# Whole V and U products for the first batch, and a new order of words for the first two batches

## The chip, the core and the metric

The kernel runs on one core of one Trainium2 chip. Its time is the device time of one execution in microseconds (us); less is better. The core's engines work side by side, each through its own list of instructions in order: TensorE (matmuls; PE in the profile), VectorE (DVE), ScalarE (ACT), GpSimd (POOL), and SyncE (SP), which here only issues transfers. An engine waits when an operand or a buffer is not ready, and everything behind the waiting instruction in its list waits too.

## The reference

Attention with grouped heads feeds a gated feed-forward block, for 8 batches of 384 tokens. There are 16 query heads and 4 key/value heads of 64 elements; the 1024 outputs of the heads of a token form its row of x.

```python
scores = scale * np.matmul(q, k.transpose(0, 1, 3, 2))
attn = np.exp(scores) / sum(...)            # softmax over keys
x = np.matmul(attn, v)  -> (batch, 384, 1024)
h = np.maximum(x @ w_in, 0.0)               # 1024 columns
u, v = h[..., :512], h[..., 512:]
v_n = (v - mean(v)) / sqrt(var(v) + 1e-6)
v_s = einsum('ts,bsd->btd', w_spatial, v_n) + b_spatial
out = (u * v_s) @ w_out
```

Inputs and outputs are 32-bit floats in device memory; the kernel multiplies in 16-bit floats and accumulates in 32 bits.

## The kernel before, in words

The work of a batch is cut into small steps, and the order in which they are issued is written out by hand as strings of words; `play` (line 641) reads a string and calls the step of each word from the table STEPS (line 592). The first list, RAMP, loads the first inputs. START (line 652) plays all of batch 0, nearly all of batch 1 and most of batch 2. STEADY (line 665) is played for each batch from 3 on, interleaving a batch with the end of the two before it. LAST finishes. The order of words fixes the order of instructions on every engine: there is no reordering behind it. A word belongs to batch 0 in START, to batch 1 with one `+`, to batch 2 with `++`, to batch 3 with `+++`.

The words, with b the batch, gp (0 or 1) the half of the heads, and t, tq, st one of three tiles of 128 tokens:

- `lq`, `lk`, `lv`: SyncE loads q of a half (line 223), k (line 178), v (line 191). `wv`, `wu`, `wo`: GpSimd issues loads, with conversion to 16 bits, of the v half of w_in's columns, its u half (line 137), and w_out (line 144); digit 0 is the first 512 rows of w_in, 1 the others. `ws` loads w_spatial and the bias, `cws` converts them on GpSimd (lines 157, 160), `tws` turns them with a transfer (line 166).
- `cq`, `ck`, `cv`: GpSimd converts q, k, v to 16 bits (lines 247, 184, 197). For batch 0 some pieces are converted on VectorE: `cqv<gp><qd><half>` (pair qd of four query heads, one half) and `ckv1` (k of the second half of the heads). The 32-bit load buffers exist once each (pool `ld`), so `lk+` can be issued only when batch 0's k has been converted, `ckv1` included.
- `K`, `Q`, `Qj`, `Qh`: TensorE turns k or some columns of q, and VectorE copies the result to SBUF (lines 278 to 297). From batch 2 on this is done by transfers: `tk` (line 263), `tq` (line 269). For batch 1, `Q10+` turns the first third of q of the second half of the heads and reads what both casts of `cq1+` wrote.
- `s<n>` (18 per batch, 9 per half of the heads): two score matmuls into two PSUM banks (line 315). `e<n>`: ScalarE's exponential of them (line 329).
- `X<gp><tq>`: 24 matmuls of attention weights and v (line 342). `N<gp><tq>`: VectorE divides by the sums and writes x (lines 356, 357).
- `T<tq>`: SyncE turns one tile of x by a transfer (line 368); `Tp<gp><tq>` does half a tile of it on TensorE, with a copy on VectorE (lines 378, 379). Batch 0 uses `Tp`, the others `T`.
- `V<st>`: x times the v half of w_in, for one tile of tokens, 8 matmuls over the 1024 rows (line 113), and then relu (line 434). `S<st>`: mean and variance (lines 447, 448). `rs`: reciprocal deviation on ScalarE (452, 453). `vn`: the three normalised tiles (line 461). `p<m>`: times w_spatial, three matmuls, and the bias added (line 492). `U<m>`: x times a quarter of the u half, 8 matmuls, and gating (line 505). `O<i>`: 4 matmuls with w_out, a copy (line 525), and for every second one a store (line 533).
- `A<st>` and `H<m>`, for batch 0 alone: the first half of V and U. Four of the eight matmuls, those over the first 512 rows, are done early; VectorE copies the half product to SBUF (lines 414, 423). The later `V` or `U` of that tile then does the other four, and VectorE adds the kept half (lines 436, 503) before relu (line 437) or gating.
- `w<n>`: n idle matmuls on a constant tile (line 303).

PSUM has 8 banks. `take1` and `take2` give a word the bank, or pair of banks, that was released longest ago; a word therefore also waits for the reader of the bank's former content.

TensorE at `V0+` waits for `T0+`. SyncE issues transfers in the order of the words: before the change `tk++ tq0++ tq1++ T0+ lk+++ lq0+++ T1+`.

Of the kernel before, what the change touches and what calls it, by code (L numbers as in the profile page):

```python
# [17 lines left out]
def kernel(  # L18
# [622 lines left out]
    def play(b, text):  # L641
# [8 lines left out]
    RAMP = """  # L650
        lqj00 lkga0 lqj01 lqd01 lt lkg1 lqd10 lv lqd11"""
    START = """
        w28 cqjv00 cka0 Qj00 w4 Ka0 w5 cqjv01 Qj01 w7 cqp011 wv0 cqv010 s0 s2 cv wv1 lk+ lq0+ Qh01 cqv100 ckv1
        cqv111 s1 e0 lq1+ ws s3 lv+ w9 s5 e2 ck+ e1 cqv101 s4 e5 e4 w6 cq0+ cqv110 s7 wu0 Q10 K1 cq1+ cws Q11
        s8 e7 e3 wu1 tws s10 lk++ s6 s9 e6 e8 lq0++ e10 X00 X01 e9 lq1++ lv++ N00 s11 N01 e11 s13 X02 e13 N02
        s12 cv+ Tp00 X10 wo e12 N10 Tp01 K0+ A0 Tp10 Q12 s14 e14 A1 V0 X11 Tp02 s15 N11 s16 K1+ A2 s17 e16
        Tp11 Q00+ S0 e15 e17 V1 X12 N12 s1+ Q10+ Q01+ Tp12 e1+ s0+ s9+ e0+ S1 e9+ s10+ ck++ H0 Q11+ Q02+ V2
        s2+ e10+ S2 e2+ s11+ rs s3+ e3+ H2 s4+ vn e11+ cq0++ H1 e4+ X00+ cq1++ tk++ N00+ p1 X10+ s5+ tq0++
        tq1++ N10+ T0+ p0 H3 e5+ U0 s12+ e12+ s7+ Q12+ U1 p2 s13+ s14+ e7+ p3 e13+ cv++ X01+ N01+ e14+ U3 s6+
        lk+++ U2 s17+ X11+ e17+ e6+ N11+ lq0+++ T1+ s8+ V0+ O4 e8+ X02+ N02+ s2++ S0+ e2++ lq1+++ s15+ O5 s0++  # L660
        e0++ s1++ O0 e15+ s16+ e16+ O2 lv+++ e1++ O1 V1+ O3 s11++ X12+ e11++ s9++ ck+++ e9++ N12+ T2+ S1+
        s10++ X00++ N00++ e10++ s14++ cq0+++ X10++ s3++ s5++ N10++ e5++ s4++ e4++ V2+ e3++ cq1+++ s13++ e14++
        tk+++ s12++ tq0+++ s8++ tq1+++ e13++ X01++ S2+ rs+ e12++ T0++ e8++ vn+ N01++ s7++ X11++ N11++ e7++ p1+
        p2+ p0+ V0++ cv+++ s15++ s17++ s6++ e6++ U0+ e15++ X02++ s16++ N02++ S0++ e17++ e16++ T1++ U1+"""
    STEADY = """
        s2 s1 e2 s0 e0 U2'' X12' p3'' N12' lq0+ cq0+ e1 lk+ s11 lq1+ e11 U3'' s9 tq0+ s10 s4 e9 e10 O0'' X00
        N00 ck+ V1' X10 S1' e4 s5 s3 T2' e5 lv+ e3 N10 O1'' V2' S2' s14 s13 s12 e13 T0 e12 O2'' O3'' X01 e14
# [45 lines left out]
```

## Time and profile before

| | |
|---|---|
| runs (median of 4; lowest to highest) | 257.55 us (256.96 to 258.83) |
| profiled execution: its time, its span | 258.83 us, 257.1 us |
| TensorE busy | 237.8 us (93%) |
| VectorE busy | 173.4 us (67%) |
| ScalarE busy | 143.7 us (56%) |
| GpSimd busy | 46.9 us (18%) |
| mean granted TensorE clock | 0.986 |

The span runs from the first to the last instruction; the profiled execution's own time has 1.7 us around it. Busy time is summed per engine. In the page's rows of slices each digit is the busy share of one fortieth of the span in tenths. A line of the timeline gives start, length, engine, line of the kernel, operation, the tiles written and read, the number of instructions, and in brackets how long the engine had been idle and what ended that. The lengths of matmuls overlap, so the time that one takes in a row is read from start to start.

### The profile page before, as it was taken

Reading aid. Unit: us, or ns where it says so; the run is one execution under the profiler, and the core shown is the slowest. Engines: PE = TensorE matmul, PEld = TensorE weight load, DVE = VectorE, ACT = ScalarE, POOL = GpSimd, SP = SyncE. Lnnn points to the kernel's source line nnn. Section 1 sums busy time; section 2 is a strip of 40 time slices with the busy share of each in tenths; the row PEclk is TensorE's granted clock in tenths of the full one; section 3 lists DMA queues with packets and bytes.
Section 4 is the critical chain, followed back from the end, with each engine's and each line's share of the span. In section 5 each row is a group of like instructions: output and inputs, shape, how many; then the busy total and the mean of one; then the engine's idle time right before and its main releaser. Section 6 shows DMA issues by size and latency. Waiting matters only on the chain.

```text
span 257.1 us, 5788 instructions
## 1 busy us (share of the span) xinstructions
PE 237.8 (93%) x2395; PEld 129.6 (50%) x2395; DVE 173.4 (67%) x350; ACT 143.7 (56%) x164; POOL 46.9 (18%) x72
## 2 busy tenths in 40 slices
PE   7779888919988999999999999999999999999993
PEld 6346435504354555455544654465446554565671
DVE  2538999913665656776677667875696667776963
ACT  3993576721669476584577474748476666800000
POOL 1615911423300061000610043003310000000000
PEclk9999999986999999999999999999999999999999
DMA  6999899989668694597977797789886325320254
GB/s 209 238 264 315 129 171 252 244 182 282 220 189 164 158 254 102 171 212 212 231 195 209 176 271 200 179 167 294 182 215 163 30 45 165 123 41 0 113 214 167
DMA packets 78042, 47.20 MB, mean 184 GB/s; under 512 B 47168, under 2 KB 74176, under 8 KB 78016
## 3 DMA queue, kind: packets, MB, share of 16 engines
q1 hardware_dynamic: 74880, 43.36, 65.5%
q0 software_dynamic: 2720, 3.15, 8.1%
q8 instruction: 18, 0.29, 0.5%
q10 hardware_dynamic: 416, 0.33, 0.4%
q14 instruction: 8, 0.07, 0.1%
HBM read 25.95 MB, written 12.58 MB: 150 GB/s over the span
## 4 chain that ended last, share of the span: by engine, by line
PE 72%; DMA 18%; POOL 4%; ACT 2%; SPq 1%; DVE 1%; issue 1%; POOLq 0%; DVEq 0%; ACTq 0%
PE banks L113 52%; DMA q<-in_q_dram 12%; PE banks L315 10%; PE banks L342 10%; DMA xT<-x 3%; POOL q L247 2%; DMA v<-in_v_dram 2%; ACT aT L329 2%; DMA k<-in_k_dram 1%; POOL setup L157 1%; POOL w_in L137 1%; POOL v L197 0%; SPq L269 0%; DVE bn L447 0%; POOL bias_tp L160 0%
## 5 line engine op out<-in xcount | busy, mean ns | idle before, releaser
L329 ACT ACTIVATE aT<-banks 128x1024 f16<-128x1024 f32 x144 | 137.8, 1025 | 77.0 <-PE banks L315 69.2
L113 PE MATMUL banks<-w_in,xT 128*128 128x512 f16 x192 | 47.4, 390 | 7.3 <-DMA xT<-x 5.7
L113 PE MATMUL banks<-w_out,gT 128*128 128x512 f16 (+1 forms) x196 | 48.0, 381 | 0.0
L342 PEld LDWEIGHTS <-aT 128*128 128x128 f16 x1152 | 40.9, 98 | 13.3 <-ACT aT L329 5.9
L113 PE MATMUL banks<-xT,w_in 128*128 128x384 f16 (+1 forms) x320 | 47.3, 294 | 0.0
L315 PE MATMUL banks<-qT,kT 64*128 64x512 f16 x288 | 44.5, 381 | 2.2 <-ACT aT L329 0.7
L342 PE MATMUL banks<-v,aT 128*128 128x65 f16 x1152 | 43.2, 193 | 3.0 <-ACT aT L329 3.0
L247 POOL CAST q<-q 128x768 f16<-128x768 f32 (+1 forms) x29 | 23.5, 837 | 103.6 <-DMA q<-in_q_dram 66.1
L525 DVE COPY osb<-banks 128x512 f32<-128x512 f32 x47 | 32.0, 687 | 10.4 <-PE banks L113 9.9
L113 PEld LDWEIGHTS <-w_in 128*128 128x128 f16 x320 | 25.6, 98 | 17.5 <-issue 5.7
L357 DVE TENSOR_TENSOR x<-banks,rec 128x512 f16<-128x512 f32 x48 | 33.2, 691 | 1.7
L434 DVE TENSOR_SCALAR v_r<-banks 128x512 f32<-128x512 f32 x21 | 14.5, 692 | 27.5 <-PE banks L113 27.5
L113 PEld LDWEIGHTS <-xT 128*128 128x128 f16 x192 | 18.3, 99 | 29.0 <-DMA xT<-x 6.9
L113 PEld LDWEIGHTS <-gT 128*128 128x128 f16 x196 | 17.1, 99 | 24.9 <-issue 10.0
L315 PEld LDWEIGHTS <-kT 64*128 64x128 f16 x288 | 12.1, 94 | 24.8 <-issue 19.0
L505 DVE SCALAR_TENSOR_TENSOR gT<-banks,vs 128x384 f16<-128x384 f32 x24 | 13.4, 558 | 11.7 <-PE banks L113 11.7
L492 DVE TENSOR_TENSOR vs<-banks,bias_tp 128x384 f32<-128x384 f32 x28 | 14.9, 553 | 6.6 <-PE banks L113 6.6
L113 PE MATMUL banks<-wsT,v_n 128*128 128x384 f16 x96 | 19.3, 326 | 0.0
L447 DVE BATCH_NORM_STATS2 bn<-v_r 128x6 f32<-128x512 f32 x24 | 16.5, 689 | 0.4
L356 DVE RECIPROCAL rec<-banks 128x8 f32<-128x8 f32 x48 | 9.7, 202 | 9.2 <-PE banks L342 8.0
L461 DVE TENSOR_SCALAR v_n<-v_r,mv,rstd 128x512 f16<-128x512 f32 x24 | 11.6, 541 | 0.8 <-ACT rstd L453 0.6
L113 PEld LDWEIGHTS <-v_n 128*128 128x128 f16 x96 | 8.0, 98 | 6.2 <-issue 2.3
(49 smaller groups left out, 91.7 us busy)
## 6 DMA issues: line engine op xcount, KB each, us to landing
out_dram<-osb SPq DMA_DIRECT2D x22, 512.0 KB, 2.9
q<-in_q_dram SPq DMA_DIRECT2D x14, 768.0 KB, 7.9
v<-in_v_dram SPq DMA_DIRECT2D x8, 384.0 KB, 4.4
k<-in_k_dram SPq DMA_DIRECT2D x7, 384.0 KB, 6.2
w_in<-in_moe_w_in_dram POOLq DMA_DIRECT2D x8, 256.0 KB, 6.7
q<-in_q_dram SPq DMA_DIRECT2D x8, 192.0 KB, 4.3
w_out<-in_moe_w_out_dram POOLq DMA_DIRECT2D x2, 512.0 KB, 12.4
out_dram<-osb SPq DMA_DIRECT2D x3, 256.0 KB, 2.1
```

The lines of the kernel that those rows point to most:

```text
L113: nc.tensor.matmul(dst[c : c + cols], w[:, c : c + cols], m, start=(i == 0), stop=(i == n - 1))
L247: engine(columns(b, gp, T["q16", b, gp])[:, js, :, half, :], T["q32", b, gp][:, half, js, :].rearrange("p j (t d) -> p j t d", t=NST),)
L315: nc.tensor.matmul(banks[:, xs[half], :], T["kT", b][lo:hi, t, gp, :], rhs[lo:hi, c * 512 : (c + 1) * 512], start=True, stop=True,)
L329: nc.scalar.activation(T["aT", b, gp, c][:, t, :, :], banks[:, x : y + 1 : y - x, :], AF.Exp, scale=scale)
L342: nc.tensor.matmul(banks[:, xs[half], j * (D + 1) : (j + 1) * (D + 1)], aT[:, t, half, o : o + P], T["v16", b][:, 2 * gp + half, t, 0 : D ...
L357: nc.vector.tensor_tensor(T["x16", b, tq][:, gp], ps[:, :, :, 0:D], rec.to_broadcast([P, 2, G, D]), ALU.mult)
L434: nc.vector.tensor_scalar(v_r, banks[:, x, :], 0.0, None, op0=ALU.max)
L447: nc.vector.bn_stats(bn, T["v_r", b, st])
L461: engine.tensor_scalar(v_n, T["v_r", b, st], T["mv", b][:, st, 0:1], T["rstd", b][:, st : st + 1], op0=ALU.subtract, op1=ALU.mult,)
L492: nc.vector.tensor_tensor(vs, f32(x, S), bias_tp, ALU.add)
L505: nc.vector.scalar_tensor_tensor(T["gT", b][:, mu, :], src, 0.0, T["vs", b, mu], op0=ALU.max, op1=ALU.mult)
L525: copy(osb[:, half * 512 : (half + 1) * 512], banks[:, x, :])
```

## The change

Only the string START is changed; RAMP, STEADY and LAST and all functions stay.

- The words A0, A1, A2, H0, H1, H2, H3 are gone. V0 to V2 and U0 to U3 of batch 0 find no kept half and do all eight matmuls in one accumulation, with relu or gating straight from PSUM, as for all other batches.
- All other words are the same ones in another order, but for the idle matmuls: w9 and w6 are gone, w3 and w22 are new.
- On SyncE the order becomes `tk++ T0+ tq0++ tq1++ lk+++ lq0+++ T1+`; for batch 2, `tk+++ T0++ tq0+++ tq1+++`; the three stores of batch 0 come in another order and lv+++ before them. GpSimd's list is the same as before. On both, the v half of w_in is loaded ahead of the u half.
- On VectorE ckv1 comes after cqv110 and cqv101 instead of after cqv100.
- On TensorE Q10+ comes ahead of V0, K0+ ahead of Tp00, O4 ahead of V0+, X10+ ahead of the first p.

```diff
     START = """
-        w28 cqjv00 cka0 Qj00 w4 Ka0 w5 cqjv01 Qj01 w7 cqp011 wv0 cqv010 s0 s2 cv wv1 lk+ lq0+ Qh01 cqv100 ckv1
-        cqv111 s1 e0 lq1+ ws s3 lv+ w9 s5 e2 ck+ e1 cqv101 s4 e5 e4 w6 cq0+ cqv110 s7 wu0 Q10 K1 cq1+ cws Q11
-        s8 e7 e3 wu1 tws s10 lk++ s6 s9 e6 e8 lq0++ e10 X00 X01 e9 lq1++ lv++ N00 s11 N01 e11 s13 X02 e13 N02
-        s12 cv+ Tp00 X10 wo e12 N10 Tp01 K0+ A0 Tp10 Q12 s14 e14 A1 V0 X11 Tp02 s15 N11 s16 K1+ A2 s17 e16
-        Tp11 Q00+ S0 e15 e17 V1 X12 N12 s1+ Q10+ Q01+ Tp12 e1+ s0+ s9+ e0+ S1 e9+ s10+ ck++ H0 Q11+ Q02+ V2
-        s2+ e10+ S2 e2+ s11+ rs s3+ e3+ H2 s4+ vn e11+ cq0++ H1 e4+ X00+ cq1++ tk++ N00+ p1 X10+ s5+ tq0++
-        tq1++ N10+ T0+ p0 H3 e5+ U0 s12+ e12+ s7+ Q12+ U1 p2 s13+ s14+ e7+ p3 e13+ cv++ X01+ N01+ e14+ U3 s6+
-        lk+++ U2 s17+ X11+ e17+ e6+ N11+ lq0+++ T1+ s8+ V0+ O4 e8+ X02+ N02+ s2++ S0+ e2++ lq1+++ s15+ O5 s0++
+        w28 cqjv00 cka0 Qj00 w4 Ka0 w5 cqjv01 Qj01 w7 cqp011 wv0 cqv010 cv wv1 lk+ s0 s2 lq0+ lq1+ w3 e0 s1 e1
+        Qh01 s4 ws cqv110 cqv101 s5 ckv1 cqv100 e2 cqv111 lv+ ck+ cq0+ e4 wu0 cq1+ w22 s8 s7 e5 e7 s6 Q11 s3
+        K1 Q10 cws s9 e6 wu1 e3 e8 tws lk++ e9 s10 lq0++ X00 X01 s11 N00 lq1++ s13 lv++ e10 N01 e11 cv+ X02
+        N02 X10 wo s12 s14 e13 N10 K0+ Tp00 Q12 e14 Tp01 e12 s15 s16 Tp10 e15 X11 Q10+ N11 V0 Tp11 K1+ s17
+        Q00+ e17 e16 Tp02 S0 V1 X12 s9+ S1 s1+ s0+ N12 e9+ s10+ e1+ Tp12 Q01+ ck++ e10+ V2 s11+ S2 s2+ e0+ s3+
+        e2+ Q11+ Q02+ s4+ rs X00+ cq0++ e11+ vn cq1++ e4+ X10+ e3+ tk++ N00+ p2 N10+ T0+ p0 s5+ s13+ s7+ e5+
+        s12+ p1 tq0++ e12+ tq1++ e7+ e13+ U0 U1 X01+ N01+ cv++ Q12+ p3 U3 s14+ s17+ U2 s6+ lk+++ e14+ lq0+++
+        e17+ X11+ s8+ e6+ N11+ T1+ e8+ O4 V0+ X02+ N02+ O2 s2++ e2++ lq1+++ O0 s1++ e1++ s16+ lv+++ O3 O1 S0+
...
```

The rest of START, to the end of batch 2's share, is reordered in the same way; the words in it are the same.

## The prediction

> **What bounds the kernel now.** I read the page's engine table and its slices first, then TensorE's waits, then the timeline of TensorE around the longest wait, then SyncE's and GpSimd's timelines to see what that wait hung on, last the busy time by stretches.
>
> ```profile
> PE 237.8 (93%) x2395; PEld 129.6 (50%) x2395; DVE 173.4 (67%) x350; ACT 143.7 (56%) x164; POOL 46.9 (18%) x72
> ...
> PE   7779888919988999999999999999999999999993
> ...
> PEclk9999999986999999999999999999999999999999
> ```
>
> TensorE is busy for 93% of the span. Its idle 19.3 us lie in the first third and in the tail: the stretches give it full business from 86 to 180 us and from 200 to 240. So the body is TensorE's own work, and the change, which alters no word after START, can win or lose only in when TensorE leaves START. That is at 90.97 us (three scores in a row, the first of STEADY). The 166.1 us behind it I take as fixed.
>
> ```profile
> PE banks L113 <- DMA xT<-x: 5.7, 1, 5.7
> PE banks L342 <- ACT aT L329: 3.0, 5, 0.9
> PE banks L113 <- DVE xT L379: 1.1, 1, 1.1
> ```
>
> One wait of 5.7 us stands out. TensorE's timeline shows it, and what it costs afterwards:
>
> ```profile
> 50.93 0.39 PE L315 MATMUL banks<-qT,kT 64*128 64x512 f16 x2
> 57.06 3.59 PE L113 MATMUL banks<-w_in,xT 128*128 128x512 f16 x8 [5.74 <-DMA xT<-x]
> 60.45 1.91 PE L113 MATMUL banks<-w_out,gT 128*128 128x512 f16 x4
> 62.15 0.95 PE L342 MATMUL banks<-v,aT 128*128 128x65 f16 x24
> ```
>
> V0+ waits until 57.06. Its 8 matmuls then take 3.39 us up to O4's start (1.73 later in the trace), and O4's 4 take 1.70 (0.97 later). The granted clock (the column after POOL's, stretches of half a microsecond) says why:
>
> ```profile
> 54.50:55.00 0.50, 0.00 (x0) 0.00 (x0) 0.00 (x0) 0.00 (x0) 0.00 (x0) 1.00 1.12 204
> 55.00:55.50 0.50, 0.00 (x0) 0.00 (x0) 0.00 (x0) 0.00 (x0) 0.00 (x0) 0.94 1.04 209
> 55.50:56.00 0.50, 0.00 (x0) 0.00 (x0) 0.00 (x0) 0.00 (x0) 0.00 (x0) 0.50 1.10 208
> ...
> 62.00:62.50 0.50, 0.50 (x11) 0.34 (x10) 0.10 (x1) 0.00 (x0) 0.34 (x1) 0.73 1.24 326
> ```
>
> It falls to half at 55.4 and is back at 62.3. This costs 1.66 + 0.73 = 2.4 us. The wait is for T0+, the transfer that turns x of batch 1's first tile. SyncE shows why it is late:
>
> ```profile
> 28.74 1.33 SPq L166 DMA_TRANSPOSE wsT<-setup  x1
> ...
> 44.02 3.92 SPq L263 DMA_TRANSPOSE kT<-k  x1
> 49.17 4.36 SPq L269 DMA_TRANSPOSE qT<-q  x2
> 53.62 1.57 SPq L368 DMA_TRANSPOSE xT<-x  x1
> ```
>
> x was complete at 43.16 (VectorE's second product for that tile). T0+ stood in SyncE's queue behind tq0++ and tq1++, and tq1++ waited for GpSimd's cast cq1++, which waited for the last q load of batch 2.
>
> **The change, part by part.**
>
> *T0+ moves ahead of tq0++ and tq1++.* Only tk++ is still before it, whose issue ends at 47.94. T0+ then lands between 47.94 + 3.4 = 51.3 (its own latency before) and 54.1, where tq0++ landed from about that place (49.17 + 4.9), because kT's transfer ahead of it landed only at 52.9 (44.02 + 8.9). I take 54.0. tq0++ and tq1++ come 1.6 us later for it. Their readers, the scores of batch 2, stand behind V0+ and five output words, so that is hidden; so is T1+, still behind tq1++ and two loads: 54.8 + 6.6 (its latency before) = 61.4, against V1+ at some 65.
>
> *A0 to A2 and H0 to H3 go.* VectorE loses lines 414, 436, 423 and 503 (2.1 + 2.1 + 2.2 + 2.2 us), and line 437's 2.7 becomes three of line 434 at 0.692: 9.2 us in all. VectorE was 92% busy from 20 to 50 us, but TensorE waited for it only 1.8 us there (1.1 for xT, 0.7 for x). The matmuls stay 8 a tile, so TensorE is given nothing back but some 0.1 us per split; what counts is that they run later. Between X10 and Q12 and up to Tp02 A0, A1 and V0 filled 0.87 + 1.74 us.
>
> *Q10+ moves ahead of V0, and nothing covers it.* X11 ended at 24.97; without these 2.6 us TensorE is at Q10+ at about 22.4. Q10+ needs cq1+:
>
> ```profile
> 21.97 1.60 POOL L247 CAST q<-q 128x768 f16<-128x768 f32 x2 [4.72 <-DMA q<-in_q_dram]
> 23.51 1.43 POOL L137 DMA_DIRECT2D w_in<-in_moe_w_in_dram  x2
> 24.94 1.61 POOL L247 CAST q<-q 128x768 f16<-128x768 f32 x2
> 26.47 2.24 POOL L157 CAST setup<-ws 128x384 f16<-128x384 f32 x3
> ```
>
> That ends at 26.55 at the earliest: a new wait of 4.1 us where there was work. Behind it in TensorE's queue stand V0, Tp11, V1, and in VectorE's the copy of Q10+, with N11 after it.
>
> *ckv1 moves behind cqv110 and cqv101.* lk+ reuses the k buffer that ckv1 reads; it was issued at 9.18, just after ckv1. cqv110 needs the second q pair, issued at 4.86 with 5.1 to landing: 9.96. Two casts and ckv1 (3 x 0.44) later it is 11.3, so lk+, lq0+, lq1+ start 2.1 us late. Ends: at 0 the engines were full anyway, at 2.1 all passes on to cq1+. The row is the stretch table: DMA share 1.06 to 1.17 in every 2 us from 8 to 22. The Trainium skill, "DMA: Bandwidth & Descriptors", Queues, rings and completion order, says that each DMA engine takes turns between the queues that have work; then GpSimd's w_in loads use what SyncE leaves, the same bytes are through by 22, and the slip would be near 0. By the issue times alone it is 2.1. SyncE's own queue was moving the q pair until 10.5, so it is empty only 10.5 to 11.3; I take 0.7. GpSimd's chain cq0+, wu0, cq1+, cws, and SyncE's tws and all behind it, slip with it. So cq1+ ends at 27.25 and the wait is 4.8 us.
>
> *From there.* Q10+ 0.3, V0 1.75: 29.3. Then VectorE sets the pace up to V2: v_r 0.69, four copies 1.6, statistics 0.87, v_r 0.69, statistics 0.87, N12 0.86 = 5.6, to 34.9; s10+, Tp12 and Q01+ 0.8; the copy of Tp12 0.4; V2 1.75: 37.8. v_r and statistics 1.56, two copies 0.8, v_n 1.46 (ScalarE's rstd lies beside the copies): 41.6. The first p starts at 41.7; before it was at 40.65. From it to the end of s8+ were 10.6 us of TensorE without a gap. Now come three H's worth more (3 x 0.70), O4 (0.97), less X10+ (0.75, now earlier) and 0.4 for the splits, plus some 0.6 for banks that wait for N10+ and vs: V0+ and O4 are through at 41.7 + 10.6 + 2.1 + 0.97 - 0.75 - 0.4 + 0.6 + 1.75 = 56.6. V0+ is reached at 54.8, and T0+ lands at 54.0 + 0.7 = 54.7: the wait is gone, the clock stays up. X02+ starts at 56.6 instead of 62.15: 5.5 us won.
>
> *The rest of START* has the same words for 28.8 us, with 2.4 us of waits (0.39, 0.49, 0.30, 0.53, 0.66), most on exponentials and banks. A changed order can make that 0.5 to 4.5; I leave it. w22, w3 instead of w9, w6: 10 more idle matmuls at 0.068 (line 303's nine took 0.61). They lie in 8.9 to 10.4, where ScalarE's exponentials, 0.93 apart from 6.83, are the pace up to X00: hidden. Without that cover they are 0.7 us.
>
> *The clock in the new wait.* Row: TensorE stopped at 51.3, and the clock fell 4.1 us later; by that a wait of 4.8 us loses it, and 2.4 us with it. The Trainium skill, "TensorE: Matmul & The Clock Gate", Part 1, says that the clock is judged over free-running windows of 3.4 us; a wait of 4.8 us holds a whole one in (4.8 - 3.4)/3.4 = 4 of 10 cases (an estimate from that page). The trace's 55.4 and 62.3 are 6.9 apart, two such windows, so I follow the rule: likeliest no loss, 2.4 us kept for the range.
>
> **Sum.** 258.83 (the profiled execution; span 257.1) - 5.5 = 253.3. That execution was the slowest of four, 1.28 above the median. If its excess was the half clock alone, 253.3 stands; if it is spread, 252.0. I take 253.0, which is 4.6 under the median 257.55 (1.8%).
>
> **The rivals.**
> - *The clock falls in the wait for cq1+*: 253.0 + 2.4 = 255.4. For it speaks the 4.8 us, against it the windows.
> - *T0+ lands late all the same*, as T1+ did with 6.6 us to landing: 48.6 + 1.6 + 6.6 = 56.8 instead of 54.8: about 255, still without the half clock.
> - *Slower: the load behind cq1+.* Place: Q10+, with the whole of batch 0's V behind it. Each microsecond by which lq0+ and lq1+ land later is one on TensorE and on every transfer behind tws. It decides from 0.7 + 4.6 = 5.3 us of slip, or 2.9 with the clock lost too. If the w_in loads, 2.1 us ahead, hold the engines until they are done (they landed at 19.5 and 20.9), two q loads of 768 KB at some 300 GB/s, 2.6 us each, come after: slip 4 to 5, with the clock lost about 259.5. Against it speaks the turn-taking.
> - *More than forecast*: no slip, fewer bank waits in the rest of START: 250.8.
> - *The change does nothing*: if the three other executions had no wait at T0+, there would be little to win: 257. They lie 0.4 to 0.7% below the profiled one; without the wait and the half clock they would lie 8.1 us, 3%, below it.
>
> **How the numbers follow.** Likeliest 0.46 (251.5 to 254.5); clock lost 0.17; T0+ late 0.11; more 0.08; slower 0.12; nothing 0.06. The range 250.3 to 257.0 leaves out the slower case, the half of nothing, and some of the low end. What a measurement can tell from no change is about 0.5%, 1.3 us. Faster: 0.46 + 0.15 + 0.09 + 0.08 = 0.78; same: 0.02 + 0.02 + 0.06 = 0.10; slower 0.12.
>
> **What would show it.** Right: no wait for xT over 1 us at V0+, the clock full at 52 to 62, xT's transfer directly behind kT's on SyncE; a wait of 4 to 6 us of line 292 for GpSimd's q cast near 22 us; lk+ issued near 11.3; VectorE busy some 164 us; STEADY from about 85.5. Wrong: TensorE at V0+ later than 57, STEADY from 90 or later, or new waits of several microseconds between 57 and 85.

## The result, and the profile after

The changed kernel takes 255.89 us (median of 43 executions, 252.36 to 258.44); the kernel before, in 64 executions beside it, takes 256.31 us (253.07 to 258.87). The ratio is 0.9992, 95% interval 0.9967 to 1.0017: no difference that can be measured, where 253.0 us and a gain of 1.8% were forecast. (Ratios in this document are of the executions within 1.5% of each kernel's fastest; medians are of all executions; where the two differ, both are given.)

The profiled execution of the changed kernel took 253.93 us, its span 252.2 us. Read against the prediction it looks like a success, and that is the puzzle of this case. The engine table and the slices of the page after:

```profile
PE 236.3 (94%) x2405; PEld 130.6 (52%) x2405; DVE 165.1 (65%) x336; ACT 143.9 (57%) x164; POOL 45.8 (18%) x72
...
PEclk9999799999999999999999999999999999999998
```

VectorE lost 8.3 us, and the row of the clock has no dip any more at 51 to 64 us, but a new one in its fifth slice. TensorE's waits up to 90 us:

```profile
PE banks L292 <- POOL q L247: 2.9, 1, 2.9
PE banks L315 <- DVE x L357: 2.2, 3, 1.1
```

The 5.7 us for xT are gone, and the wait for GpSimd's cast of q that the prediction put there is the longest now. SyncE's own queue (start, length, line, operation):

```profile
41.74 4.03 SPq L263 DMA_TRANSPOSE kT<-k  x1
45.86 2.08 SPq L368 DMA_TRANSPOSE xT<-x  x1
47.99 4.87 SPq L269 DMA_TRANSPOSE qT<-q  x2
```

T0+ is issued at 45.86, directly behind the transfer of k, and lands 5.7 us later, at 51.6. TensorE's timeline at Q10+ and V0, at V0+, and at the end of START (the last line is the first three scores of STEADY):

```profile
25.73 0.61 PE L292 MATMUL banks<-ident,q 128*128 128x128 f16 x4 [2.85 <-POOL q L247]
26.13 3.29 PE L113 MATMUL banks<-w_in,xT 128*128 128x512 f16 x8
...
55.10 1.89 PE L113 MATMUL banks<-w_in,xT 128*128 128x512 f16 x8
56.83 0.89 PE L342 MATMUL banks<-v,aT 128*128 128x65 f16 x24
...
85.23 1.09 PE L315 MATMUL banks<-qT,kT 64*128 64x512 f16 x6
```

V0+ no longer waits, X02+ follows at 56.83, and START is left at 85.23, where 85.5 was forecast. So in this one execution START ends 5.7 us earlier than in the profiled execution of before, and the two executions are 4.9 us apart (253.93 and 258.83). The medians differ by 0.4 us. The profiled execution of before stands 2.5 us above its kernel's median, that of the changed kernel 2.0 us below its own: most of the 4.9 us lies in which executions were profiled. The experiments ask what each part of the change does to the time.

### The profile page after: what moved, and what is told of

Same layout as the page of the kernel before. It is cut to its first block, busy times and chain, and to the rows that moved or that the text cites. A ratio compares the mean times of both kernels' runs of the same rounds, so it can differ in the third digit from the quotient of the medians.

```text
span 252.2 us, 5789 instructions
## 1 busy us (share of the span) xinstructions
PE 236.3 (94%) x2405; PEld 130.6 (52%) x2405; DVE 165.1 (65%) x336; ACT 143.9 (57%) x164; POOL 45.8 (18%) x72
## 4 chain that ended last, share of the span: by engine, by line
PE 81%; DMA 6%; DVE 5%; ACT 3%; POOL 2%; issue 1%; SPq 0%; DVEq 0%; ACTq 0%
PE banks L113 56%; PE banks L315 12%; PE banks L342 12%; DMA q<-in_q_dram 5%; ACT aT L329 2%; DMA xT<-x 1%; DVE bn L447 1%; POOL q L247 1%; DVE x L357 1%; PE banks L292 1%; DVE v_r L434 1%; POOL w_in L137 1%; DVE osb L525 1%; DVE rec L356 0%; PE banks L378 0%
## 5 line engine op out<-in xcount | busy, mean ns | idle before, releaser
L113 PE MATMUL banks<-w_in,xT 128*128 128x512 f16 x192 | 46.8, 388 | 1.0 <-ACT aT L329 1.0
L113 PE MATMUL banks<-w_out,gT 128*128 128x512 f16 (+1 forms) x196 | 47.1, 376 | 0.0
L113 PE MATMUL banks<-xT,w_in 128*128 128x384 f16 (+1 forms) x320 | 46.6, 294 | 0.0
L247 POOL CAST q<-q 128x768 f16<-128x768 f32 (+1 forms) x29 | 22.9, 817 | 100.3 <-DMA q<-in_q_dram 82.7
L434 DVE TENSOR_SCALAR v_r<-banks 128x512 f32<-128x512 f32 x24 | 16.6, 692 | 20.0 <-PE banks L113 20.0
L505 DVE SCALAR_TENSOR_TENSOR gT<-banks,vs 128x384 f16<-128x384 f32 x28 | 15.6, 558 | 14.3 <-PE banks L113 14.3
```

Source lines behind the costliest of these rows:

```text
L113: nc.tensor.matmul(dst[c : c + cols], w[:, c : c + cols], m, start=(i == 0), stop=(i == n - 1))
L247: engine(columns(b, gp, T["q16", b, gp])[:, js, :, half, :], T["q32", b, gp][:, half, js, :].rearrange("p j (t d) -> p j t d", t=NST),)
L434: nc.vector.tensor_scalar(v_r, banks[:, x, :], 0.0, None, op0=ALU.max)
L505: nc.vector.scalar_tensor_tensor(T["gT", b][:, mu, :], src, 0.0, T["vs", b, mu], op0=ALU.max, op1=ALU.mult)
```

## Experiments

Each was timed beside the kernel before on the same chip; rows with different times in the column "before beside it" are of different chips and times. "START left" is the start of the first scores of STEADY in the profiled execution, "rest" is its span minus that. The number of idle matmuls (the words w) is listed because it turned out to matter.

| kernel | idle | median us (n) | before beside it | of medians | ratio, 95% | START left | rest |
|---|---|---|---|---|---|---|---|
| before (the profile shown ahead) | 59 | | | | | 90.97 | 166.1 |
| before_again | 59 | 254.89 (1) | 256.57 | | | 87.29 | 165.8 |
| t0_first | 59 | 252.97 (6) | 256.57 | -1.4% | 0.9884, 0.9799 to 0.9968 | 85.50 | 165.8 |
| t0_again | 59 | 252.94 (22) | 256.17 | -1.3% | 0.9934, 0.9901 to 0.9966 | 84.44 | 165.8 |
| no_half | 59 | 256.80 (22) | 256.57 | +0.1% | 1.0022, 0.9982 to 1.0063 | 88.03 | 166.1 |
| t0_no_half | 59 | 252.79 (6) | 256.98 | -1.6% | 0.9876, 0.9824 to 0.9927 | 84.16 | 168.1 |
| t0_ckv1_late | 59 | 253.22 (6) | 256.98 | -1.5% | 0.9880, 0.9833 to 0.9927 | 86.21 | 166.0 |
| head_b_tail_a | 59 | 252.86 (6) | 257.02 | -1.6% | 0.9879, 0.9824 to 0.9933 | 83.19 | 166.6 |
| after (profile above) | 69 | 255.89 (43) | 256.31 | -0.2% | 0.9992, 0.9967 to 1.0017 | 85.23 | 167.0 |
| after_again | 69 | 254.82 (1) | 257.02 | | | 84.52 | 168.5 |
| head_a_tail_b | 69 | 255.82 (14) | 257.02 | -0.5% | 0.9977, 0.9937 to 1.0017 | 85.53 | 170.3 |
| q10_later | 69 | 256.88 (22) | 256.57 | +0.1% | 0.9991, 0.9947 to 1.0036 | 88.06 | 168.7 |
| ckv1_early | 69 | 255.14 (6) | 256.98 | -0.7% | 0.9893, 0.9820 to 0.9966 | 86.84 | 166.8 |
| both | 69 | 255.50 (22) | 256.98 | -0.6% | 0.9946, 0.9916 to 0.9976 | 85.37 | 170.7 |
| stores_late | 69 | 257.32 (22) | 257.02 | +0.1% | 1.0015, 0.9971 to 1.0059 | 88.09 | 166.4 |
| after_w12 | 59 | 254.18 (22) | 256.89 | -1.1% | 0.9953, 0.9920 to 0.9985 | 85.52 | 166.3 |
| after_w2 | 49 | 254.12 (22) | 256.17 | -0.8% | 0.9982, 0.9957 to 1.0006 | 85.16 | 166.8 |
| after_w32 | 79 | 255.01 (22) | 256.17 | -0.5% | 0.9998, 0.9963 to 1.0032 | 85.36 | 167.8 |
| t0_w19 | 69 | 255.20 (22) | 256.89 | -0.7% | 0.9939, 0.9889 to 0.9988 | 83.90 | 167.9 |

### Was the long wait in the other executions of before, too?

before_again is the kernel before, unchanged.

> The kernel before once more, unchanged, to see its T0+ wait in another execution. Theory A (the profiled execution of before was an unlucky one; usually the last q load of batch 2 lands earlier): TensorE's wait for xT near 51 us is under 3 us, the clock is not lost there, time 253 to 256. Theory B (the wait is always there, and the changed kernel pays for its loss elsewhere): a wait of 5 to 6 us again, time 256 to 259.

Its timeline of TensorE, at V0+ and at the end of START:

```profile
54.28 3.56 PE L113 MATMUL banks<-w_in,xT 128*128 128x512 f16 x8 [2.83 <-DMA xT<-x]
57.66 1.04 PE L113 MATMUL banks<-w_out,gT 128*128 128x512 f16 x4
58.54 0.89 PE L342 MATMUL banks<-v,aT 128*128 128x65 f16 x24
...
87.29 0.82 PE L315 MATMUL banks<-qT,kT 64*128 64x512 f16 x6
```

The wait is there, but 2.83 us instead of 5.74, as theory A has it; against A the clock is lost all the same, and the eight matmuls of V0+ run at half speed (3.38 to the next start), while O4 no longer does. START is left 3.7 us earlier than in the execution that the forecast was built on. That one, at 258.83 us, was among the slowest of before: the highest of the 64 is 258.87. before_again, at 254.89, lies below the median of 256.31, and the forecast's execution 2.5 us above it. So of the 5.5 us forecast some 2.5 us (against the median) to 3.7 us (against before_again) belonged to that execution and not to the kernel. no_half, below, has the same queue order at T0+, and a wait of 3.88.

### T0+ alone

t0_first is the kernel before with one word moved.

```diff
-s5+ tq0++ tq1++ N10+ T0+ p0
+s5+ N10+ T0+ tq0++ tq1++ p0
```

> The kernel before with one thing moved: T0+ ahead of tq0++ and tq1++ in SyncE's list. Theory A: the wait is mostly absent anyway, so 0 to 1 us is won (ratio 0.996 to 1.000). Theory B: 4 to 6 us are won (ratio 0.977 to 0.985).

By the medians it gains 1.4%, between the two theories; repeated later as t0_again, with 22 executions, 1.3%, 3.2 us. By the ratios the gains are 1.2% and 0.7%; the two intervals, 0.9799 to 0.9968 and 0.9901 to 0.9966, are both below 1.

> The kernel before with only the load of x for the next batch ahead of the two of q, once more, beside the other counts on this chip: 252.5 to 253.5, no wait of L113 for xT near 180. If it comes to 255 or more, the gain that it showed was the chip's and not the order's.

TensorE in t0_again, at V0+:

```profile
51.76 1.90 PE L113 MATMUL banks<-w_in,xT 128*128 128x512 f16 x8 [1.01 <-DMA xT<-x]
53.49 1.03 PE L113 MATMUL banks<-w_out,gT 128*128 128x512 f16 x4
54.35 0.90 PE L342 MATMUL banks<-v,aT 128*128 128x65 f16 x24
```

T0+ is still waited for, 1.0 us here and 2.3 us in t0_first's profile, but X02+ starts at 54.35, 4.2 us ahead of before_again. One moved word gives more than the whole change does. Then the question turns round: what in the rest of the change takes the gain back, some 3 us by the medians and 1.5 us by the ratios of t0_again and the change?

### The half products

no_half takes A0 to A2 and H0 to H3 out of the kernel before, and moves nothing. V and U of batch 0 then do all eight matmuls in one accumulation.

```diff
-Tp01 K0+ A0 Tp10 Q12 s14 e14 A1 V0 X11
+Tp01 K0+ Tp10 Q12 s14 e14 V0 X11
...
```

> The kernel before without the words A0 to A2 and H0 to H3 and nothing else: V and U of batch 0 in one accumulation. Theory A: TensorE loses work that it did while it waited for casts and exponentials, so 1 to 3 us are lost up to V0+, of which the T0+ wait hides a part: ratio 1.000 to 1.008. Theory B: the whole of it disappears in the wait at T0+, ratio 0.998 to 1.002.

The engine table of no_half:

```profile
PE 236.7 (93%) x2395; PEld 130.4 (51%) x2395; DVE 164.8 (65%) x336; ACT 143.7 (57%) x164; POOL 46.2 (18%) x72
```

VectorE is 8.6 us less busy than before and nothing comes of it: +0.1%. t0_no_half takes the same words out of t0_first, where a shorter wait for T0+ can swallow less of a gain.

```diff
-K0+ A0 Tp10 Q12 s14 e14 A1 V0
+K0+ Tp10 Q12 s14 e14 V0
...
```

> The kernel before with T0+ first, and without A0 to A2 and H0 to H3. Theory E: TensorE still waits some 2 us for T0+ there, so the loss is hidden, ratio 0.986 to 0.992. Theory F: 2 to 4 us are lost, ratio 0.996 to 1.004.

252.79 beside t0_first's 252.97: neither gain nor loss. What the half products cost VectorE, TensorE was not waiting for. In t0_no_half's profiled execution the last store landed late: 6.2 us lie behind the last matmul instead of 4.0, which is why its "rest" is long.

### The late cast, and Q10+ moved forward

t0_ckv1_late adds to t0_first the order of casts on VectorE that the change has; ckv1_early takes it out of the changed kernel.

```diff
-Qh01 cqv100 ckv1 cqv111 s1 ... cqv101 ... cqv110
+Qh01 cqv110 cqv101 ckv1 cqv100 cqv111 s1 ...
```

> The kernel before with T0+ first (which won 1.2%), and of the changed kernel's head one thing more: VectorE's casts of batch 0 in its order, so that ckv1 stands behind cqv110 and cqv101 and lk+, lq0+, lq1+ are issued some 2 us later. Theory E (the later loads are what costs): 2 to 3 us of the gain are lost, ratio 0.996 to 1.002. Theory F (the lost cover of the half products costs): at most 0.7 us, ratio 0.986 to 0.992.

```diff
-Qh01 s4 ws cqv110 cqv101 s5 ckv1 cqv100 e2
+Qh01 s4 ws cqv100 ckv1 s5 cqv110 cqv101 e2
```

> The changed kernel with ckv1 back behind cqv100 alone, so lk+ is issued near 9.2 us. Theory E: 2 to 3 us better than the changed kernel, ratio to before 0.987 to 0.992, the wait for GpSimd's q cast shorter by about 1 us. Theory F: 0 to 0.7 us, ratio 0.996 to 1.000.

t0_ckv1_late comes to 253.22 beside t0_first's 252.97: no loss there. ckv1_early comes to 255.14 beside the change's 255.89. Its ratio, 0.9893, lies in theory E's range, and its interval ends where that of the change begins (0.9966, 0.9967); but it rests on six executions, and the wait for the cast, which E had shorter, is 3.58 us in its profile instead of 2.85. q10_later takes Q10+ back behind s17 in the changed kernel, and "both" does that and ckv1_early's edit together.

```diff
-Tp10 e15 X11 Q10+ N11 V0 Tp11 K1+ s17 Q00+
+Tp10 e15 X11 N11 V0 Tp11 K1+ s17 Q10+ Q00+
```

> The changed kernel with one word moved: Q10+ after V0, Tp11, K1+ and s17 instead of ahead of V0. The wait for GpSimd's q cast (2.9 us in its profile, and half clock for part of V0) goes. Theory A: 2 to 3 us are won against the changed kernel, 2 to 3 also against the kernel before (ratio 0.988 to 0.993). Theory B: the wait for the cast is usually longer than in its profile and takes the clock with it, so 4 to 6 us are won (ratio 0.977 to 0.985).

> The changed kernel with ckv1 early and Q10+ behind V0, Tp11, K1+ and s17. Theory E: as ckv1_early or 1 us better, ratio 0.983 to 0.991. Theory F: 0.994 to 1.000.

q10_later does not win: 256.88. "both" comes to 255.50, 0.6% below before by the medians and 0.5% by the ratio. So shortening or removing the wait for cq1+ that the forecast made so much of does not by itself bring t0_first's gain back. Whether the late cast takes part of it in the changed kernel stays open: ckv1_early against the change and "both" against q10_later, each set against the kernel before beside it, are 0.6 and 0.7% lower by the medians, with intervals that include 0. The trace of q10_later has 1.2 us of that wait left, and shows two other stalls, both for transfers of x (TensorE's timeline at V2+ and in STEADY):

```profile
72.33 3.60 PE L113 MATMUL banks<-w_in,xT 128*128 128x512 f16 x8 [3.06 <-DMA xT<-x]
...
183.52 0.82 PE L113 MATMUL banks<-w_in,xT 128*128 128x512 f16 x3 [1.80 <-DMA xT<-x]
```

The first suggested that the stores of batch 0, which the change puts just ahead of T2+, delay it. stores_late computes the same with those three stores issued behind T2+, by a word st of its own:

```diff
-lv+++ O3 O1 S0+ s15+ O5 ... T2+ e3++
+lv+++ On3 On1 S0+ s15+ On5 ... T2+ st1 st0 st2 e3++
```

> The changed kernel with the three stores of batch 0's output (512 KB each) issued after T2+ instead of ahead of it. Theory C: T2+ no longer lands behind 1.5 MB of stores, so the late wait goes, 2 to 3 us are won against the changed kernel, ratio 0.988 to 0.993 to before, unless T0++ is now late behind the stores. Theory D: no change against the changed kernel, 0.997 to 1.002.

No gain: 257.32. But the transfers did what theory C said, its exception included (TensorE's timeline at V2+ and at V0++, the V of batch 2):

```profile
70.90 1.89 PE L113 MATMUL banks<-w_in,xT 128*128 128x512 f16 x8
...
77.76 3.37 PE L113 MATMUL banks<-w_in,xT 128*128 128x512 f16 x8 [2.65 <-DMA xT<-x]
```

T2+, now ahead of the stores, lands 3.0 us after its issue (7.4 in q10_later), and V2+ does not wait. T0++, now behind them and tk+++, lands after 5.1 us (3.2 in the changed kernel), and V0++ waits for it at half speed. The wait has moved on, and the time does not tell what it costs.

### Head and tail

The two STARTs have the same work behind them at V0+, so they can be crossed there: head_a_tail_b runs the changed kernel's words up to V0+ and then those of before, head_b_tail_a those of t0_first up to there and then the changed kernel's.

```diff
-... e6+ N11+ T1+ e8+ O4 V0+ X02+ N02+ O2 s2++ e2++ ...
+... e6+ N11+ T1+ V0+ O4 e8+ X02+ N02+ s2++ S0+ e2++ ...
```

> START cut at V0+: up to there the words of the changed kernel (without O4 and e8+), from there on those of the kernel before. Theory C: the late part of the changed kernel is what gives the gain back, so this wins 2 to 4 us against before (ratio 0.984 to 0.992). Theory D: the head loses, so no gain: ratio 0.996 to 1.004.

```diff
-... N11+ lq0+++ T1+ s8+ V0+ O4 e8+ X02+ N02+ s2++ S0+ e2++ ...
+... N11+ lq0+++ T1+ s8+ e8+ O4 V0+ X02+ N02+ O2 s2++ e2++ ...
```

> The other pairing: up to V0+ the words of the kernel before with T0+ ahead of tq0++ and tq1++ (the run that won 1.2%), with O4 and e8+ at its end, from V0+ on those of the changed kernel. Theory C: the gain of T0+ is given back here too, ratio 0.995 to 1.003. Theory D: it stays, ratio 0.984 to 0.990.

The head takes the gain, not the tail: 255.82 with the changed head, as the changed kernel itself; 252.86 with the changed tail alone, as t0_first. The two ratios lie in theory D's ranges. But head_a_tail_b leaves START at 85.53, just where t0_first does (85.50); it is 170.3 us from there to the end. What the head does comes out some 95 us later. after_again, the changed kernel profiled once more, has it too.

> The changed kernel once more, unchanged, to see its waits in another execution. Theory C (what T0+ wins is given back later: V2+ and its followers come earlier, and the transfers T1+, T2+, T0++, issued behind loads and the three stores of batch 0, are then late, in most executions): a wait of 2 to 4 us for xT between 60 and 80 us, or the wait for GpSimd's q cast longer than 2.9, time over 255. Theory D (the loss is in the head, before V0+): no wait for xT after 55 us, V0+ reached after 55.5.

It fits neither theory: no wait for xT between 55 and 85 us, and V0+ at 53.93. TensorE in after_again, and then in head_a_tail_b, in STEADY:

```profile
180.15 1.04 PE L113 MATMUL banks<-w_in,xT 128*128 128x512 f16 x4 [1.91 <-DMA xT<-x]
```

```profile
181.41 0.82 PE L113 MATMUL banks<-w_in,xT 128*128 128x512 f16 x3 [2.06 <-DMA xT<-x]
```

A load of x, issued at 174.73 and 176.42, takes 5.4 and 4.9 us where it took 3.5 in the kernel before, and TensorE stands. STEADY's words are the same in all these kernels, and so is the neighbourhood of that load in SyncE's queue. One thing in which the heads differ, and which they carry along for the rest of the program, is the number of TensorE's instructions: w22 and w3 are ten idle matmuls more than w9 and w6.

### Nothing but the number of idle matmuls

after_w12 gives the changed kernel before's number, t0_w19 gives t0_first the changed kernel's.

```diff
-cq1+ w22 s8 s7
+cq1+ w12 s8 s7
```

> The changed kernel with w22 as w12: ten idle matmuls fewer, so that TensorE's list has as many instructions as before the change. Theory G (what START wins is lost in the body: the ten additional idle matmuls shift where in the body TensorE's instructions are fetched, so that the fetch falls into the transfer of x near 175 us, TensorE waits 2 us for it and often loses the clock): the transfer lands in 3.5 us as in all kernels with 59 idle matmuls, no wait for xT in the body, ratio to before 0.984 to 0.990. Theory H (the body's wait is chance, and the head is simply no better): as the changed kernel, ratio 0.996 to 1.001.

```diff
-lv+ w9 s5
+lv+ w19 s5
```

> The kernel before with T0+ first, and w9 as w19: ten idle matmuls more, 69 as in the changed kernel. Theory G: the fetch falls into the same transfer of x near 175 us, a wait of about 2 us there in about half of the executions, so 1 to 3 us of the gain go, ratio 0.993 to 1.000. Theory H: at most 0.7 us for the matmuls themselves, ratio 0.986 to 0.991.

after_w12 is 1.7 us below the changed kernel (254.18, 255.89), t0_w19 is 2.2 to 2.3 us above t0_first and t0_again (255.20). Each set against the kernel before beside it, since these runs were made at different times, the differences are 0.9% (95% interval 0.4 to 1.3, drawing the executions anew with replacement) and, t0_w19 against t0_again, 0.6% (0.1 to 1.2). By the ratios nothing is shown: the first pair differs by 0.4% with intervals that overlap (0.9992, 0.9953), the second not at all (0.9939, 0.9934). after_w12's ratio falls between the two theories; t0_w19's lies in G's range, but so does that of t0_again, without the ten matmuls. t0_w19 leaves START at 83.90, earlier than both; in its STEADY stands the wait that t0_first does not have:

```profile
179.25 1.90 PE L113 MATMUL banks<-w_in,xT 128*128 128x512 f16 x8 [1.94 <-DMA xT<-x]
```

If the ten matmuls cost by their own time, each further ten would cost alike, and in START. after_w2 and after_w32 (the same word with 2 and 32) ask that.

> The changed kernel with 49 idle matmuls instead of 69 (w22 becomes w2). Theory G (the count of TensorE's instructions sets where its instruction fetches fall among the transfers; with the packet inside the transposing load of x near 175 us, T2+'s neighbour, that load takes 5 us instead of 3.5 and TensorE waits 2 us for it): the packet moves later still, to some 5 to 6 us after the issue, so the load takes 3.5 us, no wait of L113 for xT near 180, and the median is as that of 59 idle matmuls, 253.5 to 254.5. Rival H (it is the time of the idle matmuls themselves at 9 to 11 us, which the wait there does not cover): each ten fewer win the same, so about 252 to 252.5, and START is left 1.5 us earlier than with 59. If the wait near 180 is there with 49, G falls.

> The changed kernel with 79 idle matmuls (w22 becomes w32). Theory G: the packet moves about 1.5 us earlier against the load of x near 175 us, to 1 to 1.5 us after its issue, still inside it: load 4.4 to 5.4 us and a wait of L113 of 1 to 2 us near 180 in the profiled execution, median 255.5 to 257.0 (the ten further idle matmuls lie partly on the path, up to 0.6 us). Rival H: 257 to 258 with START left 1 to 2 us later and no wait near 180. If the load takes 3.5 us and the median is below 255, G falls.

With 49, 59, 69 and 79 the medians are 254.12, 254.18, 255.89 and 255.01, and START is left at 85.16, 85.52, 85.23 and 85.36: no price per matmul, and none in START. By the medians beside before, 79 stands 0.35% above 49, with an interval from -0.1 to 0.9: that pair alone would not decide, and 255.01 lies just under what G gave for 79. The wait is there with 79 and not with 49. Without it, and with it (after_w12, then after_w32, the same place):

```profile
179.02 1.89 PE L113 MATMUL banks<-w_in,xT 128*128 128x512 f16 x8
```

```profile
180.41 1.90 PE L113 MATMUL banks<-w_in,xT 128*128 128x512 f16 x8 [1.38 <-DMA xT<-x]
```

Over all the profiled executions, most of them of different kernels: with 69 or 79 idle matmuls that load took 4.9 to 5.4 us in six of nine, each time with a wait of 1.4 to 2.1 us behind it; with 49 or 59 it took 3.5 us in ten of ten. In the kernels that differ from one another by the number alone the wait is there in three of four with 69 or 79 (after_again, after_w32 and t0_w19, not after) and in none of four with 49 or 59 (after_w2, after_w12, t0_first, t0_again). In head_a_tail_b and "both" the wait, of 2.06 and 2.08 us, halved the clock for 3.4 us as well, and their rests are the longest. The rest behind START is 168.2 us on average in the nine (166.4 to 170.7) and 166.3 in the ten (165.8 to 168.1, the last with the late store).

What connects a number of matmuls at 10 us with a load at 175 us? The table of DMA queues has two of the kind "instruction"; one of them, q8, has 18 or 19 packets of 16 KB in the whole program. The packet near that load starts 5.5 us after the load's issue with 49 idle matmuls, 4.4 to 4.9 us after it in seven of the nine executions with 59 (3.0 and 3.1 in the two others), 2.3 to 3.3 with 69 and 2.1 with 79: it comes earlier the more instructions lie ahead. The DMA row of the 5 us from the issue (busy share and GB/s, 0.125 us a digit), in after_w32 and in after_w12, both issued at 175.40:

```profile
DMA  9999999999999999991900000000005999999999
GB/s 219 213 207 223 203 215 213 217 221 184 172 201 212 230 227 121 281 209 20 41 0 0 0 2 6 8 10 8 10 10 127 283 289 285 351 387 381 252 344 326
...
q8 instruction: 1, 0.02, 1.2%
```

```profile
DMA  9999999999999999999999739925858999964602
GB/s 211 215 201 223 199 221 217 227 213 168 190 213 181 211 223 209 217 207 211 217 180 191 140 103 129 160 68 184 209 184 270 356 369 387 338 197 147 199 6 66
```

With the packet (1.2% of 16 engines for 5 us, so 0.96 us on one) inside the load, all else is through after 2.5 us and for over a microsecond almost nothing moves; then the next transfer starts. Without it the load runs through. This fits a piece of the load that stands behind the packet on one DMA engine. A packet inside is not enough: eleven of the nineteen executions have one at 2.1 to 3.3 us, and of these six have the long load, one took 3.7 us and four 3.5 (before, t0_ckv1_late, after, stores_late). The packet's own time goes the other way: 0.92 to 0.98 us in all six with the long load, but 1.9 in before and t0_ckv1_late, 1.5 in after and 1.1 in ckv1_early, the one with 3.7 (read as above, a share of 2.4% in before and 1.9% in after). So where the load came through in time, it was mostly the packet that took longer; stores_late, 0.97 us and a load of 3.5, fits neither. What decides which of the two waits stays open.

That the wait in STEADY goes with the number of idle matmuls is what the profiled executions show. What it costs, 0.4 to 1.3% in the changed kernel, is shown by the medians alone, and the ratios do not confirm it. That the packet is the cause is argued from its place and its time.

## Why the prediction was wrong

**T0+ ahead of tq0++ and tq1++: right.** Landed 51.6, forecast 54.7; no wait at V0+, and full clock there. Alone it gains 3.2 to 3.6 us by the medians (0.7 to 1.2% by the ratios), and no other kernel's edit adds to it beyond the noise.

**Half products: right.** 8.3 us of VectorE (forecast 9.2), and no time by themselves, as the working had it.

**Q10+ and the wait for cq1+: right in kind, too long in size.** 2.85 us at 22.9 to 25.7, forecast 4.8 from 22.4. GpSimd's cast, the third line here, ended at 25.67 and not at 27.25 (GpSimd in the changed kernel):

```profile
21.10 1.60 POOL L247 CAST q<-q 128x768 f16<-128x768 f32 x2 [1.47 <-DMA q<-in_q_dram]
22.64 1.43 POOL L137 DMA_DIRECT2D w_in<-in_moe_w_in_dram  x2
24.07 1.60 POOL L247 CAST q<-q 128x768 f16<-128x768 f32 x2
```

**The slip of lk+ to lq1+: right, added to a wrong base.** lk+ was issued at 11.34 (forecast 11.3), and the q cast ended 0.9 us earlier than in the profiled execution of before, not 0.7 later. But that execution's 26.55 was late: over the ten profiled executions with ckv1 early the cast ends at 24.2 to 27.0, on average 25.35, over the nine with ckv1 late at 25.3 to 26.9, on average 25.97. So the slip is 0.6 us on average, with ranges that overlap, and the step that failed is the 26.55 it was added to. The lower of the forecast's ends, 0, which followed from the turn-taking of the queues in the Trainium skill, "DMA: Bandwidth & Descriptors", Queues, rings and completion order, was nearer than the upper, 2.1; no trace here shows the turns themselves. The cast order alone moved no median by more than 0.8 us, in t0_ckv1_late and in ckv1_early.

**The clock in the new wait: wrong, and the rule with it.** The forecast gave a wait of 4.8 us four chances in ten to lose the clock, by the Trainium skill, "TensorE: Matmul & The Clock Gate", Part 1: a whole free-running window of 3.4 us must be idle. The measured wait was 2.85 us, shorter than a window, and lost it all the same (the changed kernel in stretches of half a microsecond, the clock after POOL's column):

```profile
25.00:25.50 0.50, 0.00 (x0) 0.00 (x0) 0.00 (x0) 0.00 (x0) 0.50 (x1) 1.00 1.10 207
25.50:26.00 0.50, 0.27 (x3) 0.27 (x4) 0.00 (x0) 0.00 (x0) 0.50 (x2) 0.55 1.05 171
...
28.50:29.00 0.50, 0.50 (x2) 0.15 (x1) 0.00 (x0) 0.00 (x0) 0.50 (x2) 0.54 0.18 39
29.00:29.50 0.50, 0.50 (x7) 0.34 (x6) 0.04 (x1) 0.00 (x0) 0.50 (x1) 1.00 1.07 211
```

Half speed from 25.55 to 29.0, 3.4 us, the page's length: that half of the rule agrees. In after_again the same wait, of 2.89 us, kept the clock. Over all nineteen profiled executions, from 20 us on, 16 of the 17 waits of TensorE from 2.06 to 5.74 us lost it, and none of the 22 waits from 1.0 to 1.94 us did. V0 takes 3.13 us to the next start with the loss and 1.73 without: 1.4 us. The wait, shorter than forecast by 1.95, paid for that.

**START as a whole: right, in part by luck, since these two errors cancel.** V0+ at 55.10 (54.8), X02+ at 56.83 (56.6), STEADY at 85.23 (85.5).

**The base: the first step that failed.** The sum started from 258.83 and asked only whether that execution's excess was "the half clock alone" or "spread". The execution lay 2.5 us above the median of 64 (256.31). In the profiles the excess lies in START, in the very wait that the change removes: START left at 90.97, against 87.29 and 88.03 in before_again and no_half; the rest is the same within 0.3 us. The rival in which the change does nothing was set aside with the argument that without the wait and the half clock the other executions would lie 8.1 us lower. That left out the middle, which is what before_again shows: half the wait, and half speed for V0+ alone. From the mean of before_again and no_half, 87.7, to the mean of the changed kernel's two, 84.9, START wins 2.8 us, half of the forecast; with the 90.97 in the mean it would be 3.9.

**"The 166.1 us behind it I take as fixed": the second step that failed.** In the kernel before it was 166.1 and 165.8, in the changed kernel's two profiled executions 167.0 and 168.5, and in the nine with as many or more idle matmuls 168.2 on average, 1.9 us more than in the ten others. The w words were costed where they stand ("hidden", 0.7 us without cover), and there they are hidden; what they could do to the rest of the program was not asked. The first of the two has no wait in STEADY; 0.6 us of its longer rest lie behind the last matmul (4.6 us to the end, 4.0 in before). The longer rest is measured; that it comes from the w words is likely by the experiments above and not shown. 2.8 - 1.9 leaves a gain of 0.9 us; the medians show 0.4, and the ratio's interval reaches from 0.85 us of gain to 0.44 of loss (0.9967 and 1.0017 of 256.31).

**What is not settled.** Whether the changed head costs anything beside the idle matmuls. after_w12 has 1.2 us more than t0_first and t0_again (254.18; 252.97, 252.94), but against the kernel before beside each it is 0.2% more than t0_again, with an interval from -0.2 to 0.6. In the profiles X02+ starts at 56.83, 55.66, 57.12, 55.79 and 56.96 in after, after_again, after_w12, after_w2 and after_w32, on average 1.4 us later than in t0_first, t0_again and t0_w19 (56.75, 54.35, 54.05), which points to a cost. The wait for cq1+ and the late cast are the candidates; the wait was taken away, and the cast moved back, only in kernels with 69 idle matmuls, whose wait in STEADY can hide the answer.

The smallest edit is enough for the gain: before with T0+ moved takes 252.94 us against 256.17 and beats both kernels of this case. head_b_tail_a and t0_no_half, at 252.86 and 252.79 in six executions each, can't be told from it.

## What to carry to other kernels

Before you build a sum on one profile, look where its execution stands among the timed ones and profile the kernel again if it is near an end: the wait you want to remove may be what made it slow. Test a change that reorders much word by word, since its one good move may be paying for the others. And when a stage that was not touched gets longer, ask what it shares with the edit; here the number of instructions ahead of it is the likely answer.

## What the runs showed of the hardware that was not expected

- Ten idle matmuls of 0.06 us each at 10 us, hidden where they stand, went with a wait of 1.4 to 2.1 us for a load 165 us later, in six of nine profiled executions against none of ten without them. By the medians they cost 1.7 us in one kernel and 2.2 us in another, by the ratios nothing clear; twenty did not cost more than ten (255.01 against 255.89).
- Waits of TensorE of 2.06 us (head_a_tail_b) and more halved the granted clock, for 3.4 us in most cases, in 16 cases of 17; in none of 22 cases did a wait of 1.0 to 1.94 us do so.
- Executions of the same program spread over 6 us (253.07 to 258.87), and two profiles of it had the same wait at 5.74 and 2.83 us.
